# Sums of four value rows: four accumulating matmuls and a ScalarE copy in place of two GpSimd additions, for the first four units, with 1024 fewer filler columns behind each

## The chip, the cores and the metric

One core of one Trainium2 chip runs the whole program. The metric is device time in microseconds (us) of one execution; the number given for a kernel is the median of several executions. The engines are TensorE (PE; its weight loads are shown apart as PEld), VectorE (DVE), ScalarE (ACT), GpSimd (POOL) and SyncE (SP), which issues all loads and stores here. Each works through its own list of instructions in order; the order was fixed when the program was built.

## The reference

An attention with two parts feeds two feed-forward networks. Cut to what matters here:

```python
# q, k, v: (2 batches, 8 heads, 576 positions, 64)
v_d = v.reshape(B, H, 144, 4, D).mean(axis=3)       # also q_d, k_d
out_d = softmax(q_d k_d^T / 8) v_d                  # then each row repeated 4 times
out_local = softmax(q k^T / 8 where |i-j| < 4) v
x = out_d_repeated + out_local                      # -> (1152, 512)
x = (s * relu(x @ w_in)**2 + b) @ w_out             # 512 -> 2048 -> 512
out = sum_e p_e * (relu(x @ w1[e]) @ w2[e])         # 4 experts, 512 -> 1024 -> 512
```

The change is in how the sums of four rows of v (the mean without its factor of 1/4) are made.

## The kernel before

Attention is cut into 16 units. `unit(u)` is a group g (a batch and one half of the positions) and a pair of heads j; NP = 4 pairs make a group, so units 0 to 3 are the first half of batch 0, units 4 to 7 its second half, 8 to 15 the same for batch 1. k and v are loaded and reduced only by the units of a first half (hf == 0), that is units 0 to 3 and 8 to 11; the second half uses `kT{j}`, `kd{j}` and `vd{j}` again.

A unit passes through eight steps, each in a later turn of the loop at L1139. In turn i the loop emits `b_step(i-1)`, `a_step(i)`, `k_step(i)`, `d_step(i-3)`, `c_step(i-2)`, `x_step(i-3)`, `norm_step(i-1)` and `v_step(i-1)`, then the loads of later units.
- `a_step` transposes k and q on TensorE (L504, L522); ScalarE copies them out (L510, L529), VectorE sums four columns of q (L536).
- `k_step` sums four columns of kT on GpSimd (L549, L551).
- `b_step` makes the scores (L586, L601, L614 or L624), their maxima on VectorE (L625, L627) and the exponentials on ScalarE (L581).
- `norm_step` divides by the sums on VectorE (L640 to L645).
- `c_step` transposes the probabilities (L667); ScalarE copies them out (L670).
- `v_step` makes `vd{j}`, the sums of four rows of v, on GpSimd: `pool_v` adds the two upper fours of each 256 values onto the lower (L484, tile v of 72 x 512) and then the rest (L485, 72 x 256). The tile v4 has 72 partitions, and in each, for two heads a and two halves c of the positions, four rows of 64 values side by side; it has two buffers and is loaded by L430.
- `d_step` multiplies probabilities and values: L688 with `vd`, L695 with the rows of v themselves. ScalarE and VectorE add the two parts (L704, L711).
- `x_step` splits the result into a high and a low part for the networks (L723, L725).

Behind most TensorE steps stands `keep_warm`: multiplications of a tile of zeros, `idle`, in bf16, into columns of the bank that are not used (L373); b_step has its own (L594). `fill[u]` says how many columns: 1408 for units 0 to 3, 512 for 4 to 9, none after. In d_step of units 0 to 3 there are 192 free columns in the bank, so 1408 columns are 8 instructions.

Beside attention the weights of the network's first block are made ready in pieces (`prep`: L157 and L196 on ScalarE, L161, L167, L175, L186 and L199 on VectorE), and its products are started early (L777 clears two PSUM banks, L781 multiplies) and later carried on (L326). They use the pool `psm`, which has three PSUM banks; attention has five of its own (`psa`). GpSimd's instructions run in the order in which they are written. On the other engines a scheduler orders them when the program is built: by the order written, with `a_step` and `b_step` of the first units ahead, and by when it takes an instruction to be ready.

After attention the networks fill the rest (L326, L982).

Of the kernel before, what the change touches and what calls it, by code (L numbers as in the profile page):

```python
# [8 lines left out]
F32 = mybir.dt.float32  # L9
# [13 lines left out]
def attn_moe_moe_kernel(  # L23
# [14 lines left out]
    nc = tc.nc  # L38
    B, H, S, D = q.shape
# [3 lines left out]
    P = 128  # L43
# [7 lines left out]
    FAC = 4  # L51
    SD = S // FAC
    ND = SD // 2
    KP = 96
    KR = S // KP
    NP = H // 2
# [12 lines left out]
    psm = ctx.enter_context(tc.tile_pool(name="psm", bufs=3, space=bass.MemoryType.PSUM))  # L69
# [263 lines left out]
    ident = ap1.tile([P, P], F32, name="ident")  # L333
# [28 lines left out]
    last_pe = {}  # L362
# [7 lines left out]
    def keep_warm(ps, c0, cols):  # L370
        n = 512 - c0
        for _ in range(-(-cols // n) if n > 64 else 0):
            nc.tensor.matmul(ps[:, c0:], idle[:, :P], idle[:, :n], start=True, stop=True)  # L373
# [25 lines left out]
    loaded = {}  # L399
    st = {}  # L400
    fill = [1408 if u < NP else 512 if u < 2 * NP + 2 else 0 for u in range(NU)]
# [6 lines left out]
    def unit(u):  # L408
        g, j = divmod(u, NP)
        b, hf = divmod(g, HALVES)  # L410
        return g, j, b, hf

    def tiles(hf):

        return (0, CUT) if hf == 0 else (CUT, NTQ - CUT)
# [6 lines left out]
    def bank():  # L422
        return psa.tile([P, 512], F32, tag="a", name="psa")
# [57 lines left out]
    def pool_v(src, out):  # L481

        t = src[:, :, :, : 2 * D]
        nc.gpsimd.tensor_tensor(out=t, in0=t, in1=src[:, :, :, 2 * D :], op=ALU.add)  # L484
        nc.gpsimd.tensor_tensor(  # L485
            out=out.rearrange("n c a d -> n a c d"),
            in0=src[:, :, :, :D],
            in1=src[:, :, :, D : 2 * D],
            op=ALU.add,
        )  # L490
# [63 lines left out]
    def v_step(u):  # L554
        g, j, b, hf = unit(u)
        if hf == 0:
            vd = ap1.tile([ND, 2, 2, D], F32, tag=f"vd{j}", name=f"vd{j}")
            pool_v(loaded.pop(("v4", u)), vd)
            st["vd", j] = vd

    def b_step(u):
# [112 lines left out]
    def d_step(u):  # L674

        g, j, b, hf = unit(u)
        n0, m = tiles(hf)
        gq = m * TQ
        gd = gq // FAC
        pT = st.pop(("pT", u))  # L680
        vn = st.pop(("v", u))
        vd = st["vd", j]
        ps = bank()
        for a in range(2):
            o = slice(a * D, a * D + D)
            for c in range(2):
                i = m * P + ((c * 2 + a) if gd == GB else (a * 2 + c)) * gd
                last_pe["att"] = nc.tensor.matmul(  # L688
                    ps[o, gq : gq + gd], vd[:, c, a], pT[:, i : i + gd], start=c == 0, stop=c == 1
                )  # L690
        for t in range(m):
            for a in range(2):
                o = slice(a * D, a * D + D)
                i = t * P + a * TQ
                last_pe["att"] = nc.tensor.matmul(  # L695
                    ps[o, t * TQ : t * TQ + TQ],
                    vn[:, t, a],
                    pT[:, i : i + TQ],
                    start=True,
                    stop=True,  # L700
                )
        keep_warm(ps, gq + gd, fill[u])
        ud = ap2.tile([P, MX * TQ // FAC, 1], F32, tag="ud", name="ud")[:, :gd]
        nc.scalar.activation(  # L704
            out=ud.rearrange("p n o -> p (n o)"),
            in_=ps[:, gq : gq + gd],
            func=ACTF.Copy,
            scale=1.0 / FAC,
        )
        xg = ap2.tile([P, MX * TQ // FAC, FAC], F32, tag="xg", name="xg", bufs=1)[:, :gd]  # L710
        nc.vector.tensor_tensor(  # L711
            out=xg,
            in0=ps[:, :gq].rearrange("p (n r) -> p n r", r=FAC),
            in1=ud.to_broadcast([P, gd, FAC]),
            op=ALU.add,
        )
        st["xg", u] = xg
# [392 lines left out]
    def side_step():  # L1110
# [17 lines left out]
        (a_step, 0),  # L1128
        (k_step, 0),
        (d_step, 3),  # L1130
        (c_step, 2),
        (x_step, 3),
        (norm_step, 1),
        (v_step, 1),
    ]
    slots = []
    ahead = {a_step: 30, b_step: 60}
    last = NU + 2
    for i in range(last + 1):  # L1139
# [13 lines left out]
        for f, lag in steps:  # L1153
            u = i - lag
            if 0 <= u < NU:

                with tc.high_priority(ahead.get(f, 0)) if f in ahead and u < NP else nullcontext():
                    f(u)
            if f is x_step and u >= 0 and u % NP == NP - 1:
                slots += l1_steps(0, u // NP) + l2_steps(0, u // NP)  # L1160
                firsts.append(slots[-FC - KD])
                if u < NP:

                    for _ in range(3):
                        take_slot()
            if f is norm_step:
                for g, (wait, n_fc) in AHEAD.items():
                    for kk in range(KD - 1):
                        if g * NP + kk + 3 + wait <= i < g * NP + NP + 3:
                            for fc in range(n_fc):  # L1170
                                if (0, 0, fc // 2) in ready:
                                    ahead_products(g, kk, fc)
            if f in (k_step, c_step) and slots and i < last:
                take_slot()
            if f in (b_step, k_step, c_step, v_step):
                side_step()
            if 5 <= i <= 7 and f in (d_step, norm_step):
                side_step()
# [130 lines left out]
```

## Time and profile before

| | |
|---|---|
| Time, median of 3 executions | 679.46 us (679.28 to 679.66) |
| The profiled execution's own time | 679.31 us |
| Its span, from first instruction to last | 677.5 us |
| PE busy | 669.9 us, 99% |
| DVE busy | 444.4 us, 66% |
| ACT busy | 340.6 us, 50% |
| POOL busy | 107.7 us, 16% |

The times in the profile are of one execution; 1.8 us of its own time lie outside the span. A matmul's recorded duration contains the way through the array, so that matmuls behind one another overlap in the records; what one costs a full queue is read from the starts of the rows instead. An f32 product of the program (one call of `matmul`) stands in the trace as two MATMUL instructions; a transpose stands as one.

### The profile page before, as it was taken

How to read it: one execution, taken by the hardware profiler on the slowest of the kernel's cores; microseconds unless marked ns; L12 is line 12 of the kernel's file. 1: busy time of each engine (PE TensorE's matmuls, PEld its weight loads, DVE VectorE, ACT ScalarE, POOL GpSimd, SP SyncE). 2: the span in 40 equal slices, each digit the busy share in tenths (PEclk: the TensorE clock that was granted, in tenths of full speed). 3: DMA queues.
4: the chain of work that ended last, by engine and by line, in shares of the span. 5: the costliest groups of instructions: out<-in, count | busy, mean ns of one | idle time of the engine just before them, and what ended most of it. 6: DMA issues, size and time to landing. Idle time of an engine off the chain costs nothing.

```text
span 677.5 us, 11908 instructions
## 1 busy us (share of the span) xinstructions
PE 669.9 (99%) x4754; PEld 605.6 (89%) x4754; DVE 444.4 (66%) x787; ACT 340.6 (50%) x828; POOL 107.7 (16%) x123
## 2 busy tenths in 40 slices
PE   9999999999999999999999999999999999999998
PEld 6778888999999999989998999898988999989997
DVE  1899877899995896994535655556456366455442
ACT  3768778677858646554543334234243233333320
POOL 4531540100000050021201210211012012010000
PEclk9999999999999999999999999999999999999999
DMA  9975843311140110200211211002102012011012
GB/s 185 224 189 112 148 129 105 118 58 69 52 135 1 63 63 22 73 31 11 84 32 33 62 32 63 32 31 63 32 32 76 18 45 81 32 31 32 1 63 77
DMA packets 54311, 46.43 MB, mean 69 GB/s; under 512 B 32240, under 2 KB 42992, under 8 KB 54256
## 3 DMA queue, kind: packets, MB, share of 16 engines
q1 hardware_dynamic: 54256, 45.67, 24.9%
q8 instruction: 37, 0.61, 0.4%
q14 instruction: 18, 0.15, 0.1%
HBM read 43.31 MB, written 2.36 MB: 67 GB/s over the span
## 4 chain that ended last, share of the span: by engine, by line
PE 85%; DVE 8%; ACT 4%; issue 1%; POOL 1%; ACTq 0%; POOLq 0%; DVEq 0%
PE psm L326 42%; PE psx L982 33%; PE psx L326 5%; PE psa L373 2%; ACT pl L581 2%; DVE h L818 1%; DVE pl L642 1%; DVE cv L175 1%; DVE cv L186 1%; DVE cv L161 1%; PE psm L781 1%; ACT pd L581 1%; DVE pd L645 1%; DVE cv L167 1%; DVE w L199 1%
## 5 line engine op out<-in xcount | busy, mean ns | idle before, releaser
L326 PE MATMUL psm<-w,h 128*128 128x512 f32 (+2 forms) x876 | 209.4, 389 | 0.0
L326 PEld LDWEIGHTS psm<-w,h 128*128 128x128 f32 x876 | 159.8, 188 | 29.6
L982 PE MATMUL psx<-x,w 128*128 128x320 f32 (+1 forms) x960 | 147.1, 296 | 0.0
L982 PEld LDWEIGHTS psx<-x,w 128*128 128x128 f32 x960 | 136.4, 189 | 1.9
L982 PE MATMUL psx<-t,w 128*128 128x320 f32 (+1 forms) x720 | 118.3, 300 | 0.5 <-ACT rr L993 0.5
L982 PEld LDWEIGHTS psx<-t,w 128*128 128x128 f32 x720 | 104.2, 188 | 6.8 <-ACT rr L993 0.7
L261 POOL TENSOR_TENSOR sw<-raw 128x256 f32<-128x256 f32 x32 | 32.1, 1024 | 404.6 <-DMA raw<-in_moe_w_dram 243.0
L326 PE MATMUL psm<-h,w 128*128 128x320 f32 (+3 forms) x504 | 89.9, 326 | 0.4 <-DVE h L818 0.4
L1075 DVE SCALAR_TENSOR_TENSOR acc<-psm,pr,acc 128x512 f32<-128x512 f32 (+1 forms) x64 | 47.4, 741 | 56.4 <-PE psm L326 56.3
L326 PEld LDWEIGHTS psm<-h,w 128*128 128x128 f32 x504 | 77.7, 188 | 5.4 <-DVE h L818 0.9
L1022 DVE TENSOR_TENSOR rr<-psx,rr 128x320 f32<-128x320 f32 (+1 forms) x72 | 32.3, 456 | 40.0 <-PE psx L982 38.4
L996 ACT ACTIVATE h<-rr 128x320 fp32r<-128x320 f32 (+1 forms) x64 | 27.9, 443 | 54.8 <-DVE rr L1022 54.8
L993 ACT COPY rr<-psx 128x320 f32<-128x320 f32 (+1 forms) x80 | 31.4, 394 | 47.7 <-PE psx L982 47.6
L993 ACT COPY r<-psx 128x320 f32<-128x320 f32 (+1 forms) x48 | 19.1, 397 | 55.2 <-PE psx L982 55.0
L234 DVE TENSOR_TENSOR w<-raw,w 128x1024 fp32r<-128x1024 f32 x16 | 19.6, 1224 | 26.7 <-ACT w L231 26.7
L1022 DVE TENSOR_TENSOR r<-psx,r 128x320 f32<-128x320 f32 (+1 forms) x48 | 21.9, 456 | 20.4 <-PE psx L982 19.4
L997 DVE SCALAR_TENSOR_TENSOR h<-rr,h 128x320 fp32r<-128x320 f32 (+1 forms) x64 | 33.0, 526 | 2.3 <-ACT h L996 0.3
L373 PE MATMUL psa<-idle 128*128 128x256 bf16 (+4 forms) x202 | 29.3, 272 | 1.2 <-DVE sum L406 1.2
L277 DVE TENSOR_TENSOR w<-sw,w 128x1024 fp32r<-128x1024 f32 x20 | 24.5, 1226 | 7.9 <-ACT w L275 7.9
L326 PE MATMUL psm<-x,w 128*128 128x320 f32 (+2 forms) x180 | 29.3, 314 | 0.0
L996 ACT ACTIVATE h<-r 128x320 fp32r<-128x320 f32 (+1 forms) x32 | 14.2, 445 | 27.0 <-DVE r L1022 27.0
L326 PEld LDWEIGHTS psm<-x,w 128*128 128x128 f32 x180 | 27.0, 188 | 0.4 <-ACT pT L670 0.2
(133 smaller groups left out, 927.8 us busy)
## 6 DMA issues: line engine op xcount, KB each, us to landing
raw<-in_moe_w_dram SPq DMA_DIRECT2D x32, 512.0 KB
raw<-in_moe_w_in_dram SPq DMA_DIRECT2D x8, 1024.0 KB
raw<-in_moe_w_out_dram SPq DMA_DIRECT2D x8, 1024.0 KB
kn<-in_k_dram SPq DMA_DIRECT2D x8, 288.0 KB
v<-in_v_dram SPq DMA_DIRECT2D x8, 288.0 KB
out_dram<-acc SPq DMA_DIRECT2D x8, 256.0 KB
qn<-in_q_dram SPq DMA_DIRECT2D x8, 160.0 KB
vn<-in_v_dram SPq DMA_DIRECT2D x16, 72.0 KB
```

The lines of the kernel that those rows point to most:

```text
L234: nc.vector.tensor_tensor(out=k0[1], in0=source(), in1=f32(k0[0]), op=ALU.subtract)
L261: engine.tensor_tensor(out=operand(out), in0=operand(x), in1=operand(y), op=op)
L277: nc.vector.tensor_tensor(out=out, in0=w, in1=hi, op=ALU.subtract)
L326: nc.tensor.matmul(o, stat(ps, kk), mov(pm, kk, i), start=c == 0, stop=c == len(terms) - 1)
L373: nc.tensor.matmul(ps[:, c0:], idle[:, :P], idle[:, :n], start=True, stop=True)
L581: nc.scalar.activation(out=out, in_=ps, func=ACTF.Exp, bias=m, scale=1.0, accum_out=total)
L982: nc.tensor.matmul(ps, s_ap(n, half, a, w, kk), xt[x, pi][b][:, kk], start=opens and c == 0, stop=c == len(terms) - 1, skip_group_check=True,)
L993: nc.scalar.copy(st[out], st[name])
L996: nc.scalar.activation(out=h[0][:, halves[hf]], in_=t, func=ACTF.Relu)
L997: nc.vector.scalar_tensor_tensor(out=h[1][:, halves[hf]], in0=t, scalar=0.0, in1=f32(h[0][:, halves[hf]]), op0=ALU.max, op1=ALU.subtract,)
L1022: nc.vector.tensor_tensor(out=st[t], in0=st[name], in1=st[t], op=ALU.add)
L1075: nc.vector.scalar_tensor_tensor(out=a, in0=ps, scalar=p_e, in1=a, op0=ALU.mult, op1=ALU.add)
```

## The change

For units 0 to 3, `v_step` makes the sums by four products of v4 with the identity, one for each of the four rows of 64 values, accumulated in a bank of the pool `psm` (72 partitions, 256 columns of f32); ScalarE copies the bank into `vd`. Units 8 to 11 keep GpSimd's two additions. The fill behind d_step of units 0 to 3 goes from 1408 columns to 384: from 8 instructions of 192 columns to 2.

```diff
@@ v_step
             vd = ap1.tile([ND, 2, 2, D], F32, tag=f"vd{j}", name=f"vd{j}")
-            pool_v(loaded.pop(("v4", u)), vd)
+            v4 = loaded.pop(("v4", u))
+            if u < NP:
+                psv = psm.tile([P, 512], F32, tag="m", name="psm")[:ND, : 4 * D]
+                for r in range(FAC):
+                    last_pe["att"] = nc.tensor.matmul(
+                        psv,
+                        ident[:ND, :ND],
+                        v4.rearrange("n a c f -> n (a c) f")[:, :, r * D : r * D + D],
+                        start=r == 0,
+                        stop=r == FAC - 1,
+                    )
+                nc.scalar.copy(
+                    vd.rearrange("n c a d -> n a c d"),
+                    psv.rearrange("n (a c d) -> n a c d", a=2, c=2),
+                )
+            else:
+                pool_v(v4, vd)
             st["vd", j] = vd
@@ d_step
-        keep_warm(ps, gq + gd, fill[u])
+        keep_warm(ps, gq + gd, fill[u] - (1024 if u < NP else 0))
```

## Rows read from the trace of the kernel before

**Rows 1.** The page, part 1: busy time, share of the span, instructions.
```profile
PE 669.9 (99%) x4754; PEld 605.6 (89%) x4754; DVE 444.4 (66%) x787; ACT 340.6 (50%) x828; POOL 107.7 (16%) x123
```

**Rows 2.** Windows by stage: each engine's busy us (instructions), PE's granted clock, DMA share.
```profile
20.00:30.00 10.00, 10.00 (x129) 7.66 (x127) 9.02 (x18) 7.43 (x28) 4.97 (x5) 1.00 1.03 254
30.00:40.00 10.00, 8.80 (x103) 7.16 (x101) 9.69 (x18) 6.98 (x24) 4.84 (x5) 1.00 0.80 129
140.00:160.00 20.00, 20.00 (x125) 20.00 (x124) 18.83 (x30) 13.80 (x28) 0.00 (x0) 1.00 0.14 53
```

**Rows 3.** PE's waits, whole span: us in total, times, longest.
```profile
PE psa L373 <- DVE sum L406: 1.2, 1, 1.2
PE psm L781 <- DVE x L725: 0.8, 2, 0.6
PE psa L688 <- ACT pT L670: 0.7, 1, 0.7
...
PE psm L781 <- DVE w L199: 0.5, 1, 0.5
...
PE psa L667 <- DVE qd L536: 0.2, 1, 0.2
```

**Rows 4.** Chain that ended last, in order of time: start us, us, what.
```profile
18.56 0.46 DVE ml L625
...
38.55 2.16 PE psm L781 x15
```

**Rows 5.** PE's timeline from 26 us: start us, us, instructions merged, idle before.
```profile
26.16 0.64 PE L695 MATMUL psa<-pT,vn 72*64 72x64 f32 x16
26.73 0.83 PE L373 MATMUL psa<-idle 128*128 128x192 bf16 x8
27.40 0.60 PE L667 MATMUL psa<-ident,pl 128*72 128x128 f32 x4
27.84 0.27 PE L667 MATMUL psa<-ident,pd 128*72 128x128 f32 x1
...
31.15 0.44 PE L522 MATMUL psa<-ident,qn 80*128 80x80 f32 x4
31.43 0.41 PE L373 MATMUL psa<-idle 128*128 128x192 bf16 x3
32.52 0.46 PE L688 MATMUL psa<-pT,vd 72*64 72x64 f32 x8 [0.68 <-ACT pT L670]
...
37.15 0.94 PE L781 MATMUL psm<-x,w 128*128 128x256 f32 x3
38.55 2.16 PE L781 MATMUL psm<-x,w 128*128 128x256 f32 x15 [0.46 <-DVE w L199]
40.55 0.44 PE L522 MATMUL psa<-ident,qn 80*128 80x80 f32 x4
...
46.47 0.46 PE L688 MATMUL psa<-pT,vd 72*64 72x64 f32 x8
```

**Rows 6.** POOL's groups by shape, 0 to 70 us: busy us, mean ns, idle before.
```profile
L484 POOL TENSOR_TENSOR v<-v 72x512 f32<-72x512 f32 x4 | 6.3, 1564 | 2.0 <-DMA v<-in_v_dram 2.0
L485 POOL TENSOR_TENSOR vd<-v 72x256 f32<-72x256 f32 x4 | 4.5, 1127 | 0.3
```

**Rows 7.** POOL's timeline: the second unit's first addition, the fourth unit's last.
```profile
21.28 1.66 POOL L484 TENSOR_TENSOR v<-v 72x512 f32<-72x512 f32 x1 [2.02 <-DMA v<-in_v_dram]
...
41.18 1.06 POOL L485 TENSOR_TENSOR vd<-v 72x256 f32<-72x256 f32 x1
```

**Rows 8.** DVE's timeline: steps of weight preparation and norm_step.
```profile
19.15 0.68 DVE L161 TENSOR_SCALAR cv<-cv 128x1024 f32<-128x1024 f32 x1
19.87 0.69 DVE L167 TENSOR_SCALAR cv<-cv 128x1024 int32<-128x1024 int32 x1
...
22.08 0.90 DVE L640 TENSOR_SCALAR sum<-sum 128x7 f32<-128x7 f32 x1
...
26.99 0.17 DVE L640 TENSOR_SCALAR sum<-sum 128x7 f32<-128x7 f32 x1 [0.34 <-ACT pd L581]
...
30.56 1.52 DVE L161 TENSOR_SCALAR cv<-cv 128x1024 f32<-128x1024 f32 x1
32.11 1.10 DVE L167 TENSOR_SCALAR cv<-cv 128x1024 int32<-128x1024 int32 x1
...
40.00 1.66 DVE L167 TENSOR_SCALAR cv<-cv 128x1024 int32<-128x1024 int32 x1
```

**Rows 9.** ACT's groups by shape, 0 to 60 us: busy us, mean ns, idle before.
```profile
L670 ACT COPY pT<-psa 72x256 f32<-72x256 f32 x4 | 1.5, 365 | 0.0
```

## Prediction

> **What bounds the kernel now.** I read the page's busy times first, then the windows by stage, then TensorE's waits, and only then the chain and the timelines. The page gives TensorE 99% of the span [rows 1]. That alone proves little, since recorded matmuls overlap and part of them are zeros; so the windows come next. From 20 to 30 us, in the middle of the units that the change touches, TensorE has no recorded idle time at all, and after attention, at 140 to 160 us, again none [rows 2]. The waits of TensorE over the whole span confirm it: without the 1.2 us before its first instruction they make 3.4 us, in nine waits of which the first and the last kind are shown [rows 3]. An engine that works through its list in order and waits 3.4 us in 677 sets the time: an instruction more in its list is time at the end, unless it falls into one of those waits. The zeros are in that list too. They hide waits of TensorE for others, but they are instructions with a fixed place, and while they run nothing else does.
>
> The chain of waits seems to say otherwise. It runs through VectorE without a break from 18.56 to 38.51 us and re-enters TensorE at 38.55 [rows 4], and VectorE is 90% and 97% busy in those windows [rows 2]. The reader is to see that both hold: TensorE's list is full up to 31.7 us, and VectorE's list, which holds the preparation of the weights beside attention, comes in late at two places, 32.5 and 38.55 us [rows 5]. The two engines are nearly level there; the chain picks the one that was later by a little.
>
> **The change part by part.** *The products.* Each unit gets four f32 products of 256 columns. By the code each is one call of the kind that stands in the trace as two instructions, so 8 instructions of 256 columns for a unit, 32 in all. No row shows this shape. From above: the f32 transposes against the same identity start 0.11 us apart for 128 columns (27.40 to 27.84, four of them [rows 5]), which is 0.22 us for 256 and 32 x 0.22 = 7.0 us. The f32 products of d_step bear this rate out: 16 instructions of 64 columns in the 0.57 us from 26.16 to 26.73, where two go through different columns of the array together, so 0.07 us for 64 columns. From below: the products of the first block, whose tiles are of the faster F32R type in the code, take (40.55 - 38.55) / 15 = 0.133 us for 256 columns [rows 5], and 32 x 0.133 = 4.3 us. The new operands are plain f32 like the transposes', so I take 7.0 us. The weight loads of the identity run beside the matmuls, as those of the transposes do.
>
> *The zeros.* Eight fills of 192 columns take 27.40 - 26.73 = 0.67 us, 0.084 each [rows 5]. Six go in each of four units: 24 x 0.084 = 2.0 us off TensorE's list. ScalarE's read of the bank (L704) waits for the last of these fills, so d_step's result also comes 0.5 us sooner after its products. Net, TensorE has 7.0 - 2.0 = 5.0 us more work, and with the lower price 2.3 us more.
>
> *What of it falls into waits.* Two waits of TensorE lie in the stretch. Before 32.52 us three fills starting at 31.43 needed 0.25 us, so TensorE stood from 31.68 to 32.52, 0.84 us, of which 0.68 is recorded as idle; it waited for the probabilities of unit 1 behind the exponentials of unit 3 on ScalarE. The third unit's products belong between the transposes of unit 1 and this point, and fit into it. Before 38.55 us three products from 37.15 needed 0.4 us, so it stood 1.0 us, for a weight that VectorE brought late [rows 5]. By then TensorE is about 3 us later, and VectorE is not (see the next part), so this wait goes as well. That is 1.8 us. Of the 2.2 us that the other waits hold [rows 3], most are short chains that start at TensorE itself and move with it; I give 0.6 us of them back.
>
> *GpSimd and VectorE.* Eight GpSimd instructions go, 6.3 + 4.5 = 10.8 us of its time [rows 6]. Nobody waited for them: the last unit's sums were ready at 42.24 us [rows 7] and d_step took them at 46.47 [rows 5], the others had more room, and what stands behind them on GpSimd waits for ScalarE. But some VectorE steps were slow while they ran: L640 0.90 us against 0.17, L161 1.52 against 0.68, L167 1.10 and 1.66 against 0.69 [rows 8], in all 0.73 + 0.84 + 0.41 + 0.97 = 2.95 us. VectorE gets that back. It brings weights earlier, which is why I let the wait at 38.55 go; it shortens nothing while TensorE's list is full.
>
> *ScalarE.* Four copies of 72 x 256 out of PSUM, 0.365 us each by the same shape in c_step [rows 9], 1.5 us over some 30 us in which ScalarE is about 70% busy [rows 2]. They lie behind TensorE's products and long before d_step needs them, so I cost them at nothing; without that cover the exponentials behind a copy would move by 0.37 us each time, and TensorE with them, 1.5 us in all.
>
> *Loads and banks.* The products wait for v4 where GpSimd did. The second unit's load held GpSimd to 21.28 us [rows 7]. If the scheduler put the products earlier in TensorE's list, everything behind them, the transposes and scores of the next units, would stand until then. With the first unit's products in front, TensorE is 1.7 us later at that place, so I expect a wait of 0.2 us at most. The buffer of v4 comes free when TensorE has read it, about when GpSimd had. The bank comes from `psm`: two of its three are held by the early products of the first block, and the four uses of the third follow one another with many microseconds between.
>
> Sum against the profiled execution's own time: 679.31 + 7.0 - 2.0 - 1.8 - 0.6 = 681.9, and the median of the runs lies 0.15 above that execution, so 682.1 us.
>
> **The rivals.** A change of less than 0.2%, 1.4 us, can't be told from none here.
> - *Nothing absorbed, and the loads bite.* The two waits move along with TensorE (the third unit's products stand before the scores of unit 3, so that the exponentials and the probabilities of unit 1 come as much later), and no time comes back: 679.46 + 5.0 = 684.5 us, and up to 1 us more for each of units 1 to 3 if their products stand ahead of their loads. For it: the places are the scheduler's, which knows only its own estimate of a load. Against: VectorE's 2.95 us.
> - *All absorbed.* Every wait of the list goes, 3.4 us recorded and some 0.7 us more hidden in the modelled ends of the two that I worked out, because VectorE is now early everywhere: 679.46 + 5.0 - 4.1 = 680.4 us, no change. For it: nearly all of these waits end on VectorE or ScalarE. Against: several are latency within a unit.
> - *VectorE is the pace, and the time falls.* If TensorE's list up to 31.7 us only looks full, because its fills cover waits which VectorE's delay has made and the new products take the place of such waits rather than of work, then the end follows VectorE: 679.46 - 2.95 = 676.5 us. The point from which it decides is that the 5.0 us on TensorE are covered to more than 3.6 us with VectorE's gain still handed on. The Trainium skill speaks for this one: the page SBUF — State Buffer, section SBUF: two separate sides, has VectorE and GpSimd share a pair of ports which one holds for a whole instruction while the other is blocked. The slow steps agree with it in kind; by that rule VectorE could gain up to the whole of GpSimd's 10.8 us here, an estimate from that page's rule. Against this rival: fills are not waits, and TensorE had no gap from 20 to 31.7 us [rows 2, 5] in which VectorE's lateness could show.
>
> **How the numbers follow.** My forecast has 0.53, with a range of its own from 680.9 (half of the other waits gone too, and a little of the transitions) to 683.4 (only the wait at 38.55 and a third of a microsecond). Nothing absorbed has 0.15, all absorbed 0.18, VectorE as the pace 0.14. The predicted time is 682.1. The range goes from 679.4, below the second rival since the price of the products may lie under 7.0, to 684.6, the first rival without its loads; it leaves out the fall and the worst of the loads, somewhat under 2 in 10. Faster: 0.12, the last rival less a small part that lands near no change. Same: 0.20. Slower: 0.68.
>
> **What would show each step.** In the profile of the changed kernel there should be 32 instructions of 72 rows and 256 columns with the identity, starting 0.21 to 0.22 us apart; 24 fewer fills of 192 columns; POOL's busy time about 10.8 us lower; L161 and L167 near 0.68 us in the first 45 us, and VectorE with idle time there. TensorE's start of the first transposes of unit 4 should come some 3 us later than 31.15 us [rows 5], and the wait at d_step of unit 1 and that for the weight should be gone. From 140 us on everything should stand later by one constant. The prediction is wrong if the products cost nearer 0.13 us, if TensorE shows new idle time before them, if the zeros that clear the two banks (L777) leave their place ahead of the first transposes, which would change the start, or if the constant after 140 us is below 1.4 us though the 5.0 us are there: then more was waiting than the waits show.

## The result, and the profile after

The changed kernel takes 682.74 us (682.66 to 683.25, five executions) against 679.66 (679.28 to 680.8) for the kernel before: a ratio of 1.0056, 95% interval 1.0044 to 1.0067. It is slower by 3.8 us (3.0 to 4.6), more than the 0.2% that a measurement can tell from no change. 682.1 was forecast. The profiled execution took 683.06 us, its span is 681.3 against 677.5.

The page of the changed kernel, parts 1 and 4 (busy time and share of the span; shares of the chain that ended last):

```profile
PE 673.2 (99%) x4762; PEld 607.9 (89%) x4762; DVE 439.1 (64%) x787; ACT 341.6 (50%) x832; POOL 97.2 (14%) x115
...
PE 93%; DVE 2%; ACT 2%; DMA 1%; issue 1%; POOL 0%; ACTq 0%; DVEq 0%; POOLq 0%
```

The same line of part 4 for the kernel before:

```profile
PE 85%; DVE 8%; ACT 4%; issue 1%; POOL 1%; ACTq 0%; POOLq 0%; DVEq 0%
```

GpSimd is 10.5 us lighter and VectorE 5.3 us [rows 1], but the chain has left VectorE for TensorE. Where it goes now is seen in its pieces, in order of time (start us, us, what):

```profile
20.71 0.38 ACT kT L510
21.23 0.68 POOL tk L549
21.98 1.37 POOL kd L551
23.39 0.46 PE psa L630 x4
...
33.66 1.73 PE psm L562 x8
...
38.57 0.71 PE psm L797 x6
39.79 0.78 PE psa L617 x20
40.57 0.41 PE psa L640 x4
40.97 1.88 PE psm L562 x8
```

In the kernel before the chain went from 18.56 to 38.55 us through VectorE, with ScalarE in between, and came back to TensorE only there [rows 4]. Now it is TensorE work one piece behind another, the new products (L562) among it. TensorE's timeline gives their price (start us, us, instructions merged, idle before):

```profile
23.39 0.46 PE L630 MATMUL psa<-kd,qd 64*64 64x144 f32 x4 [0.58 <-POOL kd L551]
...
30.29 0.34 PE L373 MATMUL psa<-idle 128*128 128x192 bf16 x2
30.46 0.60 PE L683 MATMUL psa<-ident,pl 128*72 128x128 f32 x4
...
33.49 1.89 PE L562 MATMUL psm<-v,ident 72*72 72x256 f32 x8
35.22 0.44 PE L522 MATMUL psa<-ident,qn 80*128 80x80 f32 x4
35.50 0.41 PE L373 MATMUL psa<-idle 128*128 128x192 bf16 x3
35.84 0.46 PE L704 MATMUL psa<-pT,vd 72*64 72x64 f32 x8
...
38.19 0.38 PE L793 MATMUL psm<-idle 128*128 128x512 bf16 x1
38.22 1.06 PE L797 MATMUL psm<-x,w 128*128 128x256 f32 x6
...
40.90 1.95 PE L562 MATMUL psm<-v,ident 72*72 72x256 f32 x8
42.69 0.44 PE L522 MATMUL psa<-ident,qn 80*128 80x80 f32 x4
...
45.68 2.50 PE L797 MATMUL psm<-x,w 128*128 128x256 f32 x18
...
54.02 0.31 PE L602 MATMUL psa<-mask,identb 64*128 64x360 bf16 x1 [0.77 <-ACT pd L597]
```

Eight instructions from 33.49 to 35.22 are 0.216 us each, from 40.90 to 42.69 0.224. The fill behind d_step is two instructions, 0.17 us in place of 0.67 [rows 5]. The transposes of unit 4 start at 35.22, 4.07 us later than at 31.15 [rows 5], and d_step of unit 1 at 35.84 has no wait in front of it any more. The early products of the first block (L797, L781 before) have moved: the eighteen that stood at 37.15 and 38.55 [rows 5] now start at 45.68, behind d_step of unit 2. TensorE's waits over the whole span (us in total, times, longest):

```profile
PE psa L373 <- DVE sum L406: 1.2, 1, 1.2
PE psa L504 <- DMA kn<-in_k_dram: 1.0, 1, 1.0
PE psa L602 <- ACT pd L597: 0.8, 1, 0.8
PE psm L326 <- DVE h L834: 0.7, 2, 0.4
PE psa L630 <- POOL kd L551: 0.6, 1, 0.6
PE psx L998 <- ACT rr L1009: 0.5, 1, 0.5
PE psx L998 <- DVE rr L1038: 0.2, 1, 0.2
```

The waits for the probabilities of unit 1 and for VectorE's weights [rows 3] are gone, but without the 1.2 us at the start the list still makes 3.8 us, where it made 3.4. Three waits in the first 60 us are new. At the start the zeros that clear two banks have left their place (they stand at 38.19 and 45.65 now, L793), and TensorE waits for the load of k itself. At 23.39 the scores of unit 2 wait for the sums of k, and at 54.02 for a bank that the exponentials of an earlier unit still hold.

VectorE's groups by shape from 14 to 60 us (busy us, mean ns, idle before), for the steps that answer to [rows 8]:

```profile
L167 DVE TENSOR_SCALAR cv<-cv 128x1024 int32<-128x1024 int32 x4 | 3.2, 806 | 0.1
L161 DVE TENSOR_SCALAR cv<-cv 128x1024 f32<-128x1024 f32 x4 | 2.8, 692 | 3.4 <-ACT cv L157 3.4
...
L656 DVE TENSOR_SCALAR sum<-sum 128x7 f32<-128x7 f32 x6 | 1.0, 167 | 2.7 <-ACT pd L597 2.5
```

L161 and the sums' L656 are at their undisturbed length throughout, L167 three times of four (the fourth takes 1.15 us, beside a GpSimd instruction of `x_step`), and VectorE now waits 3.4 us for ScalarE in front of L161: what it gained, it spends waiting. The weight that TensorE waited for at 38.55 us [rows 5] comes no earlier for it, as VectorE's timeline shows, changed kernel first, then the kernel before:

```profile
37.42 1.23 DVE L199 TENSOR_TENSOR w<-cv,w 128x1024 fp32r<-128x1024 f32 x1 [0.19 <-ACT w L196]
37.28 1.22 DVE L199 TENSOR_TENSOR w<-cv,w 128x1024 fp32r<-128x1024 f32 x1
```

### The profile page after: what moved, and what is told of

Its sections match the earlier page's. It is cut to its first block, busy times and chain, and to the rows that moved or that the text cites. A ratio compares the mean times of both kernels' runs of the same rounds, so it can differ in the third digit from the quotient of the medians.

```text
span 681.3 us, 11930 instructions
## 1 busy us (share of the span) xinstructions
PE 673.2 (99%) x4762; PEld 607.9 (89%) x4762; DVE 439.1 (64%) x787; ACT 341.6 (50%) x832; POOL 97.2 (14%) x115
## 4 chain that ended last, share of the span: by engine, by line
PE 93%; DVE 2%; ACT 2%; DMA 1%; issue 1%; POOL 0%; ACTq 0%; DVEq 0%; POOLq 0%
PE psm L326 44%; PE psx L998 32%; PE psx L326 4%; PE psa L373 2%; PE psa L683 2%; PE psa L617 2%; PE psa L711 1%; PE psm L797 1%; PE psa L522 1%; PE psa L704 1%; PE psm L562 1%; DMA raw<-in_moe_w_in_dram 1%; PE psa L504 1%; DMA kn<-in_k_dram 1%; PE psa L602 0%
## 5 line engine op out<-in xcount | busy, mean ns | idle before, releaser
L373 PE MATMUL psa<-idle 128*128 128x224 bf16 (+4 forms) x178 | 27.6, 272 | 1.2 <-DVE sum L406 1.2
L1012 ACT ACTIVATE h<-r 128x320 fp32r<-128x320 f32 (+1 forms) x32 | 14.2, 445 | 27.7 <-DVE r L1038 27.7
```

The source lines that it names most:

```text
L1012: nc.scalar.activation(out=h[0][:, halves[hf]], in_=t, func=ACTF.Relu)
```

## The experiments

The kernels ran in three groups (e1 to e4, e5 to e8, e9 to e11), each beside runs of the kernel before, whose medians were 679.11, 679.25 and 679.12 us. Differences in us are the ratio to the kernel before times 679.2. In the table, idle is 138 us less TensorE's busy time in the window from 2 to 140 us of the profiled execution, and clock is the granted clock there; TensorE's list is the work that was added to or taken from it against the kernel before, at 0.22 to 0.224 us for a product's instruction, 0.083 for a fill of 192 columns and by rows of fills for the last three. Each kernel is scheduled anew when it is built, so beside its edit the order of other instructions can change. By the traces the order on all engines is the same, the edit aside, up to 43 us in e1 and the kernel before, up to 36 us in e2 and the changed kernel, and up to 28 us in e8 and e3; in e6 it is nearly that of the changed kernel throughout; the others part before 17 us.

| kernel | list, us | ratio (95% interval) | us | idle | clock |
|---|---|---|---|---|---|
| before | 0 | 1 | 0 | 2.94 | 1.00 |
| changed | +5.2 | 1.0056 (1.0044 to 1.0067) | +3.8 | 3.06 | 1.00 |
| e1 zeros only | -2.0 | 1.0040 (1.0026 to 1.0055) | +2.7 | 5.72 | 0.99 |
| e2 products only | +7.2 | 1.0077 (1.0064 to 1.0090) | +5.2 | 1.36 | 1.00 |
| e3 one row, no sums | 0 | 0.9990 (0.9982 to 0.9999) | -0.7 | 2.74 | 1.00 |
| e4 products twice | +12.2 | 1.0125 (1.0112 to 1.0138) | +8.5 | 1.05 | 1.00 |
| e5 own bank | +5.2 | 1.0049 (1.0036 to 1.0061) | +3.3 | 1.84 | 1.00 |
| e6 copy on VectorE | +5.2 | 1.0070 (1.0058 to 1.0082) | +4.8 | 3.14 | 1.00 |
| e7 two products of four | +1.6 | 1.0020 (1.0011 to 1.0029) | +1.4 | 2.20 | 1.00 |
| e8 e3 and fewer zeros | -2.0 | 1.0000 (0.9991 to 1.0008) | 0.0 | 5.09 | 1.00 |
| e9 changed, all zeros cut | -3.6 | 1.0119 (1.0103 to 1.0136) | +8.1 | 8.88 | 0.94 |
| e10 before, all zeros cut | -10.8 | 1.0111 (1.0095 to 1.0126) | +7.5 | 11.80 | 0.90 |
| e11 changed, half cut | +0.7 | 1.0099 (1.0081 to 1.0117) | +6.7 | 6.21 | 0.98 |

**The two parts of the change apart.** e1 is the kernel before with the fills alone:

```diff
-        keep_warm(ps, gq + gd, fill[u])
+        keep_warm(ps, gq + gd, fill[u] - (1024 if u < NP else 0))
```

> The kernel before with only the 24 fills behind d_step of units 0 to 3 taken out; GpSimd still makes the sums. If TensorE's list sets the time, 24 x 0.084 = 2.0 us come off: 677.7 us against 679.66, at least 678.3 if some of the waits they hid show again. If the fills only cover waits for VectorE and ScalarE, nothing comes off: 679.7.

Measured: 681.53 us, slower by 2.7. Taking 2.0 us of work out of TensorE's list made the kernel slower, which neither expectation allowed for. The waits of TensorE in e1 (whole span) show the first part of the reason:

```profile
PE psm L781 <- ACT acc L838: 1.2, 1, 1.2
...
PE psa L667 <- ACT pd L581: 1.1, 1, 1.1
PE psm L781 <- POOL x L725: 1.0, 1, 1.0
PE psa L688 <- ACT pT L670: 0.7, 1, 0.7
PE psm L781 <- ACT w L196: 0.5, 1, 0.5
```

The waits for pT, for the weight on ScalarE and for x on GpSimd lie before 39 us, where the order is that of the kernel before (the one for pT, at 31.50 us, is in that kernel too): TensorE reaches its places earlier and ScalarE and GpSimd do not. The two for acc and pd lie at 67.67 and 57.92 us, where the order is another. The second part is in the windows of e1 (busy us of each engine, granted clock, DMA) and its timeline:

```profile
36.00:38.00 2.00, 0.89 (x3) 0.48 (x3) 2.00 (x5) 1.81 (x4) 1.14 (x1) 1.00 0.30 59
38.00:41.50 3.50, 3.25 (x17) 3.25 (x18) 3.43 (x6) 2.33 (x14) 3.28 (x3) 0.59 0.54 49
```

```profile
38.25 3.29 PE L781 MATMUL psm<-x,w 128*128 128x256 f32 x15 [1.04 <-POOL x L725]
41.34 0.73 PE L522 MATMUL psa<-ident,qn 80*128 80x80 f32 x4
...
57.92 0.30 PE L667 MATMUL psa<-ident,pl 128*72 128x128 f32 x1 [1.13 <-ACT pd L581]
...
67.67 0.71 PE L781 MATMUL psm<-x,w 128*128 128x320 f32 x3 [1.23 <-ACT acc L838]
```

After a stretch in which TensorE was busy 0.89 of 2 us the granted clock goes to 0.59 in the mean, that is to the lower of its two levels, 1.2 GHz, for most of the next stretch. The same fifteen products take 3.09 us instead of 2.00 [rows 5]. In eight executions of e1 the granted clock was 1.000 three times, with 680.5 to 680.7 us, and 0.997 or 0.993 five times, with 681.2 to 684.9. So what is lost without the clock is some 1.5 us (680.65 against 679.11), and the clock is the rest, where it falls. Where the 1.5 us are lost is seen below, stretch by stretch.

e2 is the changed kernel with the fills as before:

```diff
-        keep_warm(ps, gq + gd, fill[u] - (1024 if u < NP else 0))
+        keep_warm(ps, gq + gd, fill[u])
```

> The changed kernel with the full 1408 columns of zeros again: the sums by TensorE and ScalarE alone. If TensorE's list sets the time, the 24 fills cost their 2.0 us once more: 684.7 against 682.74. If the zeros are cover only: 682.7.

Measured: 684.2 us, a ratio of 1.0077 against 1.0056. The intervals touch (1.0064 and 1.0067), so 1.4 us is the likeliest size and not a sure one. Here the same 24 fills go at a gain, where e1 lost by it.

**VectorE's relief by itself.** e3 is the kernel before without the sums of units 0 to 3:

```diff
-            pool_v(loaded.pop(("v4", u)), vd)
+            v4 = loaded.pop(("v4", u))
+            if u < NP:
+                nc.scalar.copy(vd.rearrange("n c a d -> n a c d"), v4[:, :, :, :D])
+            else:
+                pool_v(v4, vd)
```

> The kernel before with no sums for units 0 to 3: one ScalarE copy of the first of the four rows in their place (the other three rows are left out). GpSimd's eight additions are gone and TensorE gets nothing new, so this is what VectorE's relief alone is worth. If TensorE's list sets the time, only the waits for VectorE in the first 60 us can come back, 0 to 1 us: 678.7 to 679.7. If VectorE is the pace, 2.95 us: 676.7.

Measured: 678.38 us, faster by 0.7 (0.1 to 1.2). VectorE's groups in e3, 14 to 60 us, show that the relief is there in full:

```profile
L167 DVE TENSOR_SCALAR cv<-cv 128x1024 int32<-128x1024 int32 x4 | 2.8, 689 | 0.1
L161 DVE TENSOR_SCALAR cv<-cv 128x1024 f32<-128x1024 f32 x4 | 2.7, 684 | 1.4 <-ACT cv L157 1.4
```

The rival in which VectorE is the pace asked for 2.95 us and falls.

e8 puts e3 and the fewer fills of e1 together.

> One row copied by ScalarE in place of GpSimd's sums (the other three rows are left out) and the 24 fills out as well, so TensorE's list is shorter by 2.0 us than in the kernel before and nothing is put in. If the loss of the run with the zeros alone came from VectorE slowed by GpSimd, it is gone and the list's 2.0 us show: 676.4. If the zeros stand in for waits and for the clock, the loss stays: 679.9 to 680.8, with the granted clock under 1 in a part of the runs.

Measured: 679.29 us, the time of the kernel before, 0.7 us above e3, and 0.6 under the range for a loss. The intervals of the two overlap, so it is not sure that the fewer fills lose here; but at the end nothing of the 2.0 us is left, for which the ratio would be 0.996. The granted clock was 1.00 in all eleven executions, so the reason is waits: in the profiled ones idle time goes from 2.74 us in e3 to 5.09. Since GpSimd's sums are gone from both, that does not need a slowed VectorE.

**Where the fewer fills lose.** The first product of a unit's scores, which multiplies the mask, is a place that every kernel has. At units 6 and 9 it has the same work behind it in all six kernels of this table, the 24 fills and the new products aside (starts in the profiled executions, us):

| kernel | unit 1 | unit 6 | unit 9 | 1 to 6 | 6 to 9 |
|---|---|---|---|---|---|
| before | 13.31 | 50.15 | 77.18 | 36.84 | 27.03 |
| e1, fewer fills | 12.44 | 49.90 | 79.11 | 37.46 | 29.21 |
| e3 | 12.33 | 48.64 | 75.06 | 36.31 | 26.42 |
| e8, fewer fills | 12.82 | 47.92 | 77.11 | 35.10 | 29.19 |
| e2 | 13.36 | 56.15 | 83.39 | 42.79 | 27.24 |
| changed, fewer fills | 12.82 | 54.02 | 81.23 | 41.20 | 27.21 |

The fills that are taken out all lie between units 1 and 6. There they bring 1.2 us (e8 against e3) and 1.6 us (the changed kernel against e2) of their 2.0, with and without products beside them; in e1 the stretch is 0.6 us longer, but the lower clock behind 38 us cost 1.4 us there (1.09 in the fifteen products, 0.34 in the transposes and fills behind them), so that without it some 0.8 us would be gained. From unit 6 to unit 9 TensorE has the same instructions in all six, and there e1 and e8 lose 2.2 and 2.8 us to waits, such as the two at 57.92 and 67.67 us in e1. So what these two kernels lose with the clock up, they lose behind the place of the fills, in a stretch that the scheduler has ordered otherwise. Whether the fewer fills would lose there in the old order too was not tested; each figure is from one execution.

**How much of the products comes through.** e4 makes the four products twice, e7 makes two of the four:

```diff
-                for r in range(FAC):
+                for r in [*range(FAC)] * 2:      # e4
+                for r in range(2):               # e7, stop=r == 1
```

> The changed kernel with each unit's four products made twice (the second pass starts the sums anew, so they stay the same). If TensorE's list sets the time, 32 more instructions of 0.22 us: 7.2 us more, 689.9 against 682.74. If a good part of the products lies in waits of TensorE, clearly less: under 687.

> The changed kernel with two of the four products of each unit (rows 2 and 3 of each four are left out of the sums): 16 instructions of 0.224 us fewer, 3.6 us of TensorE's list. If all of it is time at the end: 679.2 against 682.74. If a third falls into waits, as in the run with the products twice (4.7 of 7.2 us came through): 680.4.

Measured: 687.5 and 680.21 us. From none (e8) over two and four to eight products a unit the kernel goes 0.0, +1.4, +3.8, +8.5 us, for 3.6, 7.2 and 14.2 us of work in the list. The first 3.6 us bring 1.4, the next 3.6 bring 2.4, the last 7.1 bring 4.7: a share of 0.4 at first and of two thirds later. The small first share comes with e8, which carries the loss behind unit 6: from unit 1 to unit 6 the four kernels take 35.10, 37.82, 41.20 and 46.77 us, so the steps there are 2.7, 3.4 and 5.6 us. The idle time falls over the whole way, from 5.09 to 1.05 us, but not at every step (2.20 and 3.06 between). The 687.5 us of e4 lie between its two marks.

**The new waits.** e5 gives the sums a bank of attention, e6 copies them on VectorE:

```diff
-                psv = psm.tile([P, 512], F32, tag="m", name="psm")[:ND, : 4 * D]
+                psv = bank()[:ND, : 4 * D]       # e5
-                nc.scalar.copy(
+                nc.vector.tensor_copy(           # e6
```

> The changed kernel with the sums in one of attention's five banks in place of one of the three of psm, so that the zeros that clear two banks of psm can go ahead of the first transposes again, as in the kernel before, where TensorE waits for a load anyway. If TensorE's list sets the time, their 2 x 0.21 us come off: 682.3 against 682.74. If attention's banks run short, new waits of TensorE for ScalarE and VectorE: 683 or more. If the place of these zeros is without weight: 682.7.

> The changed kernel with the copy into vd on VectorE in place of ScalarE. If the copies on ScalarE delayed the copy of kT behind them and so the wait of TensorE for kd (0.6 us recorded) is their work, it goes: 682.1 against 682.74. If that wait comes from the order of the exponentials, no change, 682.7. If VectorE is the pace, four more instructions there cost 1.6 us: 684.3.

Measured: 682.29 us for e5, the forecast size, but its interval takes in the changed kernel's time. Its profile has the zeros ahead of the first transposes again and no wait there. e6 took 683.84 us and did not lose the wait for kd, which its list of waits has at 0.7 us:

```profile
PE psa L630 <- POOL kd L551: 0.7, 1, 0.7
```

So the copies on ScalarE are not what makes it. The copy of kT that the wait goes back to stands behind the exponentials of unit 1 in the changed kernel and ahead of them in the kernel before, and the second of the two GpSimd additions that follow takes longer (timelines, the changed kernel's two lines first):

```profile
20.60 0.49 ACT L510 ACTIVATE kT<-psa 128x288 f32<-128x288 f32 x1
21.98 1.36 POOL L551 TENSOR_TENSOR kd<-tk 128x144 f32<-128x144 f32 x1
17.54 0.47 ACT L510 ACTIVATE kT<-psa 128x288 f32<-128x288 f32 x1
18.84 0.42 POOL L551 TENSOR_TENSOR kd<-tk 128x144 f32<-128x144 f32 x1
```

So the wait goes with the order that the scheduler made, which e6 keeps, and with the longer addition; the two were not tried apart. e6's 683.84 us can't be split further: the intervals of e6 and of the changed kernel overlap.

**All the zeros.** If TensorE's list were all, the other zeros of units 0 to 3 should go too. e9 is e5 with 384 columns behind each step, e10 the kernel before with the same, e11 is e5 with 896 columns (384 behind d_step):

```diff
-    fill = [1408 if u < NP else 512 if u < 2 * NP + 2 else 0 for u in range(NU)]
+    fill = [384 if u < NP else 512 if u < 2 * NP + 2 else 0 for u in range(NU)]
```

> The sums by TensorE in a bank of attention, and the zeros of units 0 to 3 cut to 384 columns behind every step, not behind d_step alone: by the rows of the kernel before some 8.8 us more off TensorE's list. If the list sets the time with the share that the products had (0.4 to 0.7), 682.3 less 3.5 to 6.2: 676.1 to 678.8, faster than both kernels. If these zeros stand in for waits and the clock as those of d_step did in the run with the zeros alone: 681 to 684, with the granted clock below 1.

> The kernel before, sums by GpSimd, with the same cut of all zeros of units 0 to 3 to 384 columns: 10.8 us off TensorE's list. If the list sets the time: about 673. If the zeros stand in for waits, no gain: 679 to 682, and more where the clock falls.

> The sums by TensorE in a bank of attention, zeros of units 0 to 3 cut to 896 columns behind each step and 384 behind d_step: some 4.5 us off TensorE's list. List with a share of 0.4 to 0.7: 679.1 to 680.5. Zeros as cover: 682 or more.

Measured: 687.26, 686.25 and 685.65 us, all slower than both kernels. That is above both ranges of e9; for e10 and e11 it falls to the second case, which had no upper end. The windows of e9:

```profile
10.00:20.00 10.00, 8.08 (x55) 5.17 (x52) 2.99 (x12) 4.79 (x25) 1.09 (x2) 0.68 1.07 213
20.00:30.00 10.00, 8.40 (x59) 5.50 (x57) 5.35 (x8) 3.74 (x7) 1.37 (x2) 0.81 0.84 190
30.00:40.00 10.00, 8.30 (x80) 5.76 (x82) 7.80 (x15) 5.57 (x22) 2.10 (x3) 0.66 0.68 181
```

TensorE runs a good part of these 30 us at its lower level. Its longest wait is for a load in front of the new products:

```profile
PE psa L562 <- DMA v<-in_v_dram: 1.9, 1, 1.9
```

That is the wait that the prediction's first rival named. Of the profiled runs only e9 and e11 have it (1.9 and 2.0 us), in which zeros are missing ahead of the products; in the changed kernel no product waited for its load. No version that was run and makes all sums is faster than the kernel before.

## Why the prediction was right

The direction, the size (2.6 us forecast, 3.8 measured in the ratio, 3.1 in the medians) and the mechanism hold. Two terms were somewhat off, both the same way, and no error made up for another. Step by step:

- *TensorE's list sets the time.* Right for work that is added: e7, the changed kernel and e4 rise with it, and the chain lies on TensorE. For work that is taken out it holds in part: in their own stretch the fills gave back 1.2 to 1.6 us of 2.0 where the clock stayed up, but e1 and e8 to e11 are no faster at the end than without the cut. The sentence "fills are not waits" in the last rival goes too far. A fill is work, but what it covers can be a wait for another engine, and without it the granted clock can fall.
- *Price of the products.* Right: 7.0 us taken, 0.216 to 0.224 us an instruction measured, 6.9 to 7.2 us for 32.
- *Price of the zeros.* 2.0 us in the list, as shown by 0.17 us against 0.67; what came off the time is about 1.4 us (e2 against the changed kernel).
- *What falls into waits.* The sum of 2.4 us was too large. With the fills kept, the products' 7.2 us came out as 5.2 (e2), so 2.0 us were absorbed; 5.2 less 1.4 is the 3.8 measured. The two waits that were worked out did go. The one at 38.55 us did not go because VectorE brings weights earlier: the weight was ready at 38.65 us, before at 38.51. TensorE came later to it, and the scheduler put the products behind d_step of unit 2 as well. That no other waits would come was the part that was off: the wait for kd and the wait for a bank, 0.6 and 0.8 us, are new.
- *Banks.* The sums did not fit in beside the zeros that clear two banks of `psm`: these zeros left their place at the start, which the prediction had named as something that would spoil it. A wait of 1.0 us for a load stands there instead, and the first transposes start at 5.40 us against 5.43, so it cost no time at that point; but the zeros, some 0.2 us each, now stand in the full part of the list, at 38.19 and 45.65. With the sums in a bank of attention (e5) they are back at the start.
- *VectorE.* The relief is real, 5.3 us of busy time, more than the 2.95 that was added up from four rows and half of the 10.8 that the last rival allowed at most, and worth 0.7 us (e3). The prediction read the chain wrongly in one point: between 18.56 and 38.51 us it is not VectorE without a break, it has ScalarE's exponentials and copies from 25.30 to 26.96 and from 29.07 to 30.54. The conclusion, that TensorE and what follows it are nearly level there, doesn't hang on it.
- *ScalarE and loads.* Costed at nothing and at 0.2 us. No product waited for a load, and the copies delayed nothing that e6 could show.
- *Later by one constant.* The span is longer by 3.8 us, and in the window from 140 to 670 us TensorE is busy 529.19 of 530 us, before 529.50: nothing came back after attention.

How the difference builds up can be followed in the two profiles. The changed kernel's first scores (L617) stand at 11.57 us, before (L601) at 12.05, so it starts 0.48 us ahead. The scores of unit 6 start 3.87 us later than before, those of unit 13 3.49 later (106.99 against 103.50). The 0.48 us go with the execution and not with the change: e2 and e6 have the changed kernel's instructions up to there, with first scores at 12.10 and 13.64 us, and in e6 the clock rose latest (last section). What stays open is how the absorbed 2.0 us divide among single waits, since old ones went, new ones came, and the order changed with them.

## What to carry to other kernels

Filler multiplications are best not priced by their own time alone. Take them out in a run of its own, and look at the clock and the waits: here 24 of them, 2.0 us of the list, were worth 1.2 to 1.6 us in their own stretch, and in e1 the lower clock took back more than they gave. A kernel that is built anew is also scheduled anew, so before a difference at the end is put down to the edit, compare the two profiles at places with the same work behind them: e1 and e8 lost 2.2 and 2.8 us where nothing had been taken out. And before work is moved off an engine because it slows a neighbour, ask whose list is full: relief for VectorE was worth 0.7 us here, and the engine that took the work over had 3 us of free time in 140.

## What the runs showed of the hardware that was not expected

A stretch of 2 us in which TensorE was busy for 0.89 was followed by one with a granted clock of 0.59 in e1, in a part of the executions only (five of eight below 1.000), and the time followed it, 680.5 to 684.9 us. With the zeros cut everywhere the granted clock from 2 to 140 us was 0.94 (e9) and 0.90 (e10), although TensorE was still busy for 129 and 126 of the 138 us there (its instructions are longer at the lower level).

All thirteen profiles begin with the same eight fills, whose starts agree to 0.01 us up to 3.73 us, at the spacing of the lower level (0.43 us for 512 columns). The spacing of the higher level comes between 3.7 and 4.1 us in the changed kernel and in e4, and only between 8.9 and 9.8 us in e6: the time of the rise differs from execution to execution. With it, and with the landing of the first load of k (the first transposes start at 4.84 us in e4, 5.55 in e6), the first scores move, from 11.01 us in e4 to 13.64 in e6.
